# Retention attention followed by a gated feed-forward block: query order, blocks of x^T kept in DRAM, and the order of loads and sums

## The chip, the cores and the metric

The kernel runs on one core of one Trainium2 chip. The core has a matrix engine (PE, TensorE; its weight loads are shown apart as PEld), a vector engine (DVE), a scalar engine (ACT), a general one (POOL, GpSimd) and a queue engine (SP) that issues most DMAs. All run on their own, each through its own instructions in order, and wait for each other by semaphores. The metric is the device time of one execution in microseconds. The kernel before took 1052.0 us (median of 8 runs, 1049.72 to 1055.76).

## What is computed

```python
# q, k, v: (8, 8, 576, 64); w_in: (512, 2048); w_out: (2048, 512)
scores = scale * np.matmul(q, k.transpose(0, 1, 3, 2))
gamma = 1.0 - 2.0 ** (-5.0 - np.arange(H, dtype=np.float32))
rel = pos[:, None] - pos[None, :]
Dmat = np.where(rel >= 0, gamma[:, None, None] ** rel[None, :, :], 0.0)
attn_out = np.matmul(scores * Dmat[None], v)
x = attn_out.transpose(0, 2, 1, 3).reshape(B * S, H * D)      # 4608 x 512
h = x @ w_in
sp = np.maximum(h, 0.0) + np.log1p(np.exp(-np.abs(h)))
g = h * erf(sp)
out = g @ w_out                                               # 4608 x 512
```

The weights come as 64-bit floats, so the kernel reads each as a pair of 32-bit words and makes a 32-bit float of it.

## The kernel before

**Attention.** The 4608 tokens are cut into 36 pieces of 128 tokens: 32 pieces of one batch each, and 4 that hold the last 64 tokens of two batches. Each piece has three stages, written as functions. `transposes(i)` (L300) brings queries and keys into columns: for the first 8 pieces (`SQUARES`) by PE and an ACT copy, later by DVE transposes of 32 x 32 blocks (L310), which read "squares" that the loads have laid out (L115), with token = 4 r + a for row r of block a. It writes both with the tokens in their own order, so the elements of one block lie 4 apart (2 apart in the 64-token pieces). `scores(i)` (L320) multiplies keys and queries and masks them on DVE. `outputs(i)` (L333) multiplies by the values, adds what the state of the batch so far gives, makes the next state (sums on DVE, decay on POOL, L384), and scales the result into the tile `x` (DVE). The values of a piece are first weighed by powers of the decay (`weigh_values`, POOL, L298). The list `stages` (L398) has the order: transposes i+1, outputs i, scores i+1, with two swaps. `attend(upto)` issues the next stages. `load(i, names)` issues the loads of a piece on SP.

**Feed-forward.** Four pieces make a chunk of 512 tokens, 9 chunks. The hidden width is worked through in 4 groups (g = 0 to 3). For each (g, c), `First` multiplies x^T by w_in and `Second` multiplies the result by w_out. Both use a Strassen-Winograd scheme of 7 products instead of 8, each product 4 matmuls of 128 x 128 by 256 (8 records, since a float32 matmul is two). The operands need sums of quarter blocks: S1, S2, S3, S4 of x (`operands_x`, L431; t1 is S1, t2 is S2, t4 stands in the place of A22, S3 takes the place of b12), sums of the weights (L194, L204), and sums of g (`sums`, L532). The first chunk of group 0 is done without the scheme (`plain`). The first group is computed while the attention still delivers x; then x tiles are stored to DRAM (`store_x`, L427; 7 blocks: four of x^T with S3 and three sums) and loaded for groups 1 to 3 (`load_x`, L422). Partial outputs go to DRAM (`od`) and come back in `begin` (L550). Products of a block share PSUM banks: `a` collects product after product, so each must be read (`take`, L568) before the next one is added into it; `e` and `g` hold the others.

**Weights.** `load_weights` issues one part (1/8 of a group, 0.5 MB). `rounding` (L226) makes 32-bit floats of it: two ACT operations, four DVE operations in five steps, two POOL operations (L259, L260), then a new `load_weights`; `round_weights(n)` advances n steps. Four raw buffers.

**Order.** Everything is issued in the order of the Python program. In the beginning a string (L655) has it, one letter a step: a is a stage of attention, p a quarter of half of the plain products, w two parts of weights, a digit so many rounding steps, s `store_x(0)`; after the first stages two dummy matmuls keep PE awake. After that the loop at L679 goes through the blocks First(1), Second(0), First(2), Second(1), ...; a Second block issues products T2, T3, T1 (`middle`), the two products of the First block after next (`first`), then B22 and T4 (`last`), and mixes stages of attention and rounding steps between them.

Of the kernel before, what the change touches and what calls it, by code (L numbers as in the profile page):

```python
# [22 lines left out]
CONST_COLS = H + NP * P + NP + P + H  # L23
# [7 lines left out]
def decays():  # L31

    gamma = 1.0 - 2.0 ** (-5.0 - np.arange(H, dtype=np.float64))
    pairs = gamma.reshape(2, NP)
    t = np.arange(P)
    gk = pairs.T.reshape(1, H) ** -t[:, None]
    row = pairs.repeat(D, axis=0)
    out = np.where(np.arange(NP) % 2 == 0, row, np.roll(row, D, axis=0))  # L40
    gq = out[:, :, None] ** t[None, None, :] / math.sqrt(D)
    gp = row**P
    tri = t[None, :] >= t[:, None]
    gk2 = gk[t % D]
    return np.concatenate([x.reshape(P, -1) for x in (gk, gq, gp, tri, gk2)], axis=1).astype(np.float32)
# [3 lines left out]
def kernel(  # L49
# [39 lines left out]
    xd = [dram.tile([P, n_dc + 3, TCH], FP32, tag="xd", name="xd") for _ in range(n_ch)]  # L89
# [18 lines left out]
    live = {}  # L108

# [45 lines left out]
    nc.scalar.dma_start(out=cst, in_=consts)  # L155
    ends = [0]
    for m in (H, NP * P, NP, P, H):
        ends.append(ends[-1] + m)
    gk, gq, gp, tri, gk2 = (cst[:, a:b] for a, b in zip(ends, ends[1:]))
    gq = gq.rearrange("p (a i) -> p a i", a=NP)  # L160
    gp = gp.unsqueeze(2).to_broadcast([P, NP, D])
    load(1)
    load(2, "kv")
# [62 lines left out]
    def rounding():  # L226


        while True:
            while not words or words[0][2] > most_g[0]:  # L230
                yield
            t, name, g, slot, j, sums = words.pop(0)
            w = operands(name, g)
            dst = w[:, slot : slot + 2, j, :]
            pairs = t[:, :].rearrange("p (h f two) -> p h f two", h=2, two=2)
            pairs_f = t[:, :].bitcast(FP32).rearrange("p (h f two) -> p h f two", h=2, two=2)
            low, high = pairs[:, :, :, 0], pairs[:, :, :, 1]
            r_f, high_f = pairs_f[:, :, :, 0], pairs_f[:, :, :, 1]
            a_f, a = dst, dst.bitcast(UINT32)
            nc.scalar.activation(a_f, high_f, AF.Abs)  # L240
            nc.scalar.mul(out=r_f, in_=low, mul=2.0**-52)
            yield


            nc.vector.tensor_scalar(
                out=a_f, in0=a_f, scalar1=HIGH_LEAST, scalar2=HIGH_MOST, op0=ALU.max, op1=ALU.min
            )
            yield
            nc.vector.tensor_scalar(
                out=a, in0=a, scalar1=3, scalar2=0x3FFFFFFF, op0=ALU.logical_shift_left, op1=ALU.bitwise_and  # L250
            )
            yield
            nc.vector.scalar_tensor_tensor(
                out=a, in0=high, scalar=0xC0000000, in1=a, op0=ALU.bitwise_and, op1=ALU.bitwise_or
            )
            yield

            nc.vector.tensor_scalar(out=high, in0=a, scalar1=0xFF800000, scalar2=None, op0=ALU.bitwise_and)  # L258
            nc.gpsimd.tensor_tensor(out=r_f, in0=high_f, in1=r_f, op=ALU.mult)  # L259
            nc.gpsimd.tensor_tensor(out=a_f, in0=a_f, in1=r_f, op=ALU.add)  # L260
            load_weights()
            yield
            if sums:
                yield from sums(*(w[:, i] for i in range(7)))
# [9 lines left out]

    tri2 = cpool.tile([P, P], FP32, name="tri2")
    nc.vector.tensor_copy(out=tri2, in_=tri)
    nc.vector.memset(tri2[:D, D:], 0.0)

# [21 lines left out]
    def transposes(i):  # L300
        t = live[i] = loaded.pop(i)
        if i < SQUARES:
            weigh_values(i + 1)
        for name in "qk":
            tT = t[name + "T"] = att.tile([P, NP, P], FP32, tag=name + "T", name=name + "T")
            if i >= SQUARES:
                for _, _, n, r0 in pieces[i]:
                    a = r0 // SQ * D
                    squares = t[name + "s"][:, :, a : a + n // SQ * D].rearrange("p h (a d) -> p h a d", d=D)
                    nc.vector.transpose(  # L310
                        out=tT[:, :, r0 : r0 + n].rearrange("p h (r a) -> p h a r", r=SQ), in_=squares[:, :, :, :SQ]
                    )
            else:
                pt = ps_at.tile([P, NP, P], FP32, tag="at", name=f"pt_{name}")
                for p in range(NP):
                    nc.tensor.transpose(pt[:, p, :], flat(t[name][:, 2 * p : 2 * p + 2, :]), ident)
                nc.scalar.copy(out=tT, in_=pt)
        load(i + 2, "q")
# [14 lines left out]
    def outputs(i):  # L333
# [5 lines left out]
        o = [ps_at.tile([P, 4, P], FP32, tag="at", name=f"o{j}") for j in range(2)]  # L339
# [10 lines left out]
        for state, r0, n in seen:  # L350
            for p in range(NP):
                for e in range(2):
                    nc.tensor.matmul(
                        o[p % 2][heads[(e + p) % 2], p // 2, r0 : r0 + n],
                        lhsT=state[heads[e], p, :],
                        rhs=t["qT"][heads[e], p, r0 : r0 + n],
# [4 lines left out]
        b, s0, n, _ = segments[0]  # L361
        if n == P:

            kv = o[0].rearrange("p a i -> p (a i)")[:, 2 * P :].rearrange("p (a d) -> p a d", a=NP)
            for p in range(NP):
                for e in range(2):
# [7 lines left out]
                    )  # L374
            sums = kv
# [9 lines left out]
            kept[b] = new  # L385
        load(i + 3, "kv")
        weigh_values(i + 1)
        c, at = i // PC, i % PC * P
        if (0, c) not in x:
            x[0, c] = x_tile()  # L390
        for j in range(2):
            by = gq[:, j::2, :n].unsqueeze(2).to_broadcast([P, 2, P // n, n])
            dst, got = (
                y.rearrange("p a (m i) -> p a m i", i=n) for y in (x[0, c][:, j:NP:2, at : at + P], o[j][:, :2])
            )
            tt(dst, got, by, ALU.mult)

    stages = [(transposes, 0), (scores, 0)]  # L398
    for i in range(len(pieces)):
        stages += [(transposes, i + 1), (outputs, i), (scores, i + 1)]  # L400
        if i in (PC - 1, PC):
            stages[-3:-1] = stages[-2], stages[-3]
# [19 lines left out]
    def load_x(g, c):  # L422
        m = n_dc + 3 if c > 0 else n_dc
        x[g, c] = x_tile()
        nc.sync.dma_start(out=x[g, c][:, :m], in_=xd[c][:, :m])

    def store_x(c):  # L427
        m = n_dc + 3 if c > 0 else n_dc
        nc.sync.dma_start(out=xd[c][:, :m], in_=x[0, c][:, :m])

    def operands_x(g, c):  # L431
# [3 lines left out]
        if g == 0 or c == 0:  # L435
# [3 lines left out]
            tt(t4, b21, t2, ALU.subtract)  # L439
        if g == 0:  # L440
            store_x(c)
        x[g, c] = {A11: b11, A12: b21, S4: b22, A22: t4, S1: t1, S2: t2, S3: b12}

    class First:
# [87 lines left out]
        def sums(self):  # L532
            g11, g21, g12, g22 = (t[:, j] for t in (self.t1, self.t2) for j in range(2))
            s1, s2, s3, s4 = (self.s[:, i, j] for i in range(2) for j in range(2))
            tt(s1, g12, g22, ALU.add)
            tt(s2, s1, g11, ALU.subtract)
            tt(s3, g11, g12, ALU.subtract)
            tt(s4, g21, s2, ALU.subtract)
# [3 lines left out]
    class Second:  # L542


        def __init__(self, first):
            self.of = first
            self.g, self.c = first.g, first.c
            self.end = (self.g, self.c) == (n_g - 1, n_ch - 1)
# [19 lines left out]
        def take(self, half, oh, acc, engine):  # L568
# [3 lines left out]
            elif engine == "scalar":  # L572
                nc.scalar.copy(out=dst, in_=acc)
            else:
                nc.vector.tensor_copy(out=dst, in_=acc)
# [5 lines left out]
        def first(self):  # L581
# [3 lines left out]
            self.take(0, 0, self.a, "scalar")  # L585
# [5 lines left out]
        def middle(self):  # L591
            self.e = ps_e.tile([P, 2, OH], FP32, tag="g", name="g2")
            self.product(T2, self.a, False)
            self.take(1, 0, self.a, "vector")
# [4 lines left out]
            self.take(1, 1, self.a, "vector")  # L599
# [3 lines left out]
        def last(self):  # L603
            self.product(B22, self.a, False)
            self.take(0, 1, self.a, "scalar")
            self.store(0)
            if self.end:
                self.store(1, slice(OH, D_MODEL))
# [3 lines left out]
            self.store(1, slice(0, OH if self.end else D_MODEL))  # L612
            yield

        def store(self, half, os=slice(0, D_MODEL)):
            if self.g < n_g - 1:
                nc.sync.dma_start(out=od[self.c][:, half, :, os], in_=self.o[:, half, :, os])
            else:
                for tp in range(2):
                    for b, s0, n, r0 in pieces[self.c * PC + 2 * half + tp]:  # L620
                        nc.sync.dma_start(
                            out=out[b * S + s0 : b * S + s0 + n, os], in_=self.o[r0 : r0 + n, half, tp, os]
                        )
# [31 lines left out]
    for j, what in enumerate("aaaawaaawaa4a1a5asa1a4pa5papapa5p4apa1p4apa5a5a"):  # L655
# [4 lines left out]
        elif what == "s":  # L660
            store_x(0)
        elif what == "w":
            load_weights()
            load_weights()
        else:
            round_weights(int(what))
        if j < 7 and what == "a":
            keep_busy(2)
    firsts[0].softplus()
    most[0] = before_chunk(3)  # L670
    attend(after_chunk(1))
    operands_x(0, 1)
    attend(done[0] + 1)
# [4 lines left out]
    firsts[0].multiply()  # L678
    for b, nxt in zip(blocks[1:], blocks[2:] + [None]):  # L679
        n = order.index((b.g, b.c))  # L680
        if isinstance(b, First):
            most_g[0] = order[n - 1][0] + 1
            seconds[n - 1].begin()
            if n + 1 < n_s and order[n + 1][0] > 0:
                load_x(*order[n + 1])
# [5 lines left out]
        elif n + 2 < n_s:  # L691
            f = firsts[n + 1]
            for step, _ in enumerate(b.middle()):
                attend(min(done[0] + 1, most[0]))
                if step == 0:
                    f.erf()
            if n + 2 < n_ch:
                attend(after_chunk(n + 2))
            operands_x(*order[n + 2])
            run(nxt.first(), (1,))  # L700
            f.multiply()
            run(b.last(), (0, 1))
        elif n + 1 < n_s:
            firsts[n + 1].erf()
            seconds[n + 1].begin()
            run(b.middle())
            firsts[n + 1].multiply()
            run(b.last())
            firsts[n + 1].sums()
            run(nxt.first())  # L710
        else:
            run(b.middle())
            run(b.last())
# [30 lines left out]
```

## Time and profile before

| | |
|---|---|
| median of 8 runs | 1052.0 us |
| the profiled execution | 1052.88 us, its span 1051.1 us |
| PE busy | 1023.1 us (97%) |
| weight loads of PE | 878.7 us (84%) |
| DVE busy | 641.6 us (61%) |
| ACT busy | 378.5 us (36%) |
| POOL busy | 133.6 us (13%) |
| moved by DMA | 192.23 MB, mean 183 GB/s |
| store of one x tile | 1792 KB, 8 of them |
| load of one x tile | 1792 KB, 24 of them, median 10.9 us to landing; 3 of 1024 KB, 9.4 us |
| output stores | 43, at most 256 KB, 2.4 us to landing |

The profile is one execution. Busy shares are means over the whole span, and the kernel has stages with different limits, so the shares of a stage and the idle time in front of single instructions say more than the table. In rows of the timeline the bracket at the end is the idle time of the engine before the instruction and what ended it. PE's clock can be granted in part; a matmul then takes longer without any idle time.

### The profile page before, as it was taken

Reading aid. Unit: us, or ns where it says so; the run is one execution under the profiler, and the core shown is the slowest. Engines: PE = TensorE matmul, PEld = TensorE weight load, DVE = VectorE, ACT = ScalarE, POOL = GpSimd, SP = SyncE. Lnnn points to the kernel's source line nnn. Section 1 sums busy time; section 2 is a strip of 40 time slices with the busy share of each in tenths; the row PEclk is TensorE's granted clock in tenths of the full one; section 3 lists DMA queues with packets and bytes.
Section 4 is the critical chain, followed back from the end, with each engine's and each line's share of the span. In section 5 each row is a group of like instructions: output and inputs, shape, how many; then the busy total and the mean of one; then the engine's idle time right before and its main releaser. Section 6 shows DMA issues by size and latency. Waiting matters only on the chain.

```text
span 1051.1 us, 15730 instructions
## 1 busy us (share of the span) xinstructions
PE 1023.1 (97%) x6322; PEld 878.7 (84%) x6322; DVE 641.6 (61%) x1001; ACT 378.5 (36%) x459; POOL 133.6 (13%) x130
## 2 busy tenths in 40 slices
PE   8789999999999999999999999999999999999997
PEld 7668887787788888888888888888888888888885
DVE  3679888778687654556655655555556544454444
ACT  3233232231331444443433333434443333333341
POOL 2551331221221100100001000110100000000000
PEclk9879999999999999999999999999999999999999
DMA  9989979989996534544455455554343444454432
GB/s 195 250 175 242 242 185 256 213 228 238 215 260 177 190 110 150 190 170 170 159 197 198 153 188 206 190 191 150 150 150 121 150 170 176 165 199 174 167 121 80
DMA packets 146777, 192.23 MB, mean 183 GB/s; under 512 B 96016, under 2 KB 121104, under 8 KB 138640
## 3 DMA queue, kind: packets, MB, share of 16 engines
q1 hardware_dynamic: 146560, 190.88, 61.4%
q8 instruction: 50, 0.82, 0.3%
q10 hardware_dynamic: 144, 0.34, 0.1%
q14 instruction: 23, 0.19, 0.1%
HBM read 137.70 MB, written 53.48 MB: 182 GB/s over the span
## 4 chain that ended last, share of the span: by engine, by line
PE 72%; DMA 6%; DVE 6%; SPq 4%; issue 1%; DVEq 0%; ACT 0%
PE a L559 21%; PE a L453 19%; PE g L453 10%; PE g L559 10%; PE e L559 5%; PE e L453 5%; SPq L123 2%; DMA raw_qs<-in_q_dram 2%; DMA raw_v<-in_v_dram 1%; DVE t L93 1%; DMA raw_ks<-in_k_dram 1%; SPq L137 1%; DVE x L93 1%; PE s L326 1%; DVE o L93 1%
## 5 line engine op out<-in xcount | busy, mean ns | idle before, releaser
L453 PE MATMUL a<-x,wa 128*128 128x256 f32 x1120 | 267.8, 382 | 0.0
L453 PEld LDWEIGHTS a<-x,wa 128*128 128x128 f32 x1120 | 212.7, 191 | 29.9 <-issue 0.2
L559 PE MATMUL a<-wb,s 128*128 128x256 f32 x864 | 205.6, 381 | 2.1 <-DVE o L93 2.1
L559 PEld LDWEIGHTS a<-wb,s 128*128 128x128 f32 x864 | 162.9, 190 | 26.1 <-DVE o L93 2.4
L93 DVE TENSOR_TENSOR o<-a,o 128x512 f32<-128x512 f32 x108 | 74.4, 689 | 108.3 <-PE a L559 104.0
L93 DVE TENSOR_TENSOR t<-g,t 128x512 f32<-128x512 f32 x70 | 48.3, 690 | 147.6 <-ACT t L483 112.5
L453 PE MATMUL g<-x,wa 128*128 128x256 f32 x560 | 133.4, 381 | 0.4 <-DVE o L93 0.3
L453 PEld LDWEIGHTS g<-x,wa 128*128 128x128 f32 x560 | 105.5, 190 | 16.4 <-DVE o L93 1.6
L259 POOL TENSOR_TENSOR wraw<-wraw 128x512 f32<-128x512 f32 x32 | 33.5, 1047 | 459.5 <-DVE wraw L258 242.4
L478 ACT COPY t<-a 128x512 f32<-128x512 f32 x35 | 20.5, 587 | 186.8 <-PE a L453 186.8
L93 DVE TENSOR_TENSOR t<-t,s 128x1024 f32<-128x1024 f32 x72 | 87.2, 1253 | 0.0
L522 ACT ACTIVATE s<-t 128x1024 f32<-128x1024 f32 x72 | 72.1, 1049 | 36.3 <-DVE t L93 36.3
L489 ACT COPY t<-a 128x512 f32<-128x512 f32 x35 | 20.5, 586 | 149.7 <-PE a L453 149.7
L559 PE MATMUL g<-wb,s 128*128 128x256 f32 x288 | 69.6, 385 | 3.1 <-DVE t L93 3.1
L526 ACT ACTIVATE s<-s 128x1024 f32<-128x1024 f32 x72 | 72.1, 1049 | 0.4
L559 PE MATMUL a<-wb,t 128*128 128x256 f32 x288 | 68.6, 381 | 0.0
L559 PE MATMUL e<-wb,t 128*128 128x256 f32 x288 | 68.6, 381 | 0.0
L559 PE MATMUL g<-wb,t 128*128 128x256 f32 x288 | 68.2, 380 | 0.0
L453 PE MATMUL e<-x,wa 128*128 128x256 f32 x280 | 66.9, 382 | 0.0
L559 PEld LDWEIGHTS g<-wb,s 128*128 128x128 f32 x288 | 54.9, 192 | 11.0 <-DVE t L93 3.4
L559 PEld LDWEIGHTS g<-wb,t 128*128 128x128 f32 x288 | 54.6, 190 | 7.5
L559 PEld LDWEIGHTS e<-wb,t 128*128 128x128 f32 x288 | 54.3, 190 | 7.7
(77 smaller groups left out, 1175.2 us busy)
## 6 DMA issues: line engine op xcount, KB each, us to landing
x<-xd SPq DMA_DIRECT2D x24, 1792.0 KB, 10.9
od<-o SPq DMA_DIRECT2D x54, 512.0 KB, 4.2
o<-od SPq DMA_DIRECT2D x27, 1024.0 KB, 7.2
xd<-x SPq DMA_DIRECT2D x8, 1792.0 KB, 7.5
raw_qs<-in_q_dram SPq DMA_DIRECT2D x96, 112.0 KB, 5.0
raw_ks<-in_k_dram SPq DMA_DIRECT2D x96, 112.0 KB, 4.5
raw_k<-in_k_dram SPq DMA_DIRECT2D x64, 128.0 KB, 4.5
raw_v<-in_v_dram SPq DMA_DIRECT2D x64, 128.0 KB, 4.7
```

Of the source, the lines that this page charges most:

```text
L93: nc.vector.tensor_tensor(out=out, in0=in0, in1=in1, op=op)
L123: nc.sync.dma_start(out=t[part * SQ : (part + 1) * SQ, :, at : at + m - SQ], in_=tokens[:, :, d0 : d0 + m - SQ])
L137: nc.sync.dma_start(out=t[r0 : r0 + n, e::2, :], in_=heads.rearrange("h p d -> p h d"))
L259: nc.gpsimd.tensor_tensor(out=r_f, in0=high_f, in1=r_f, op=ALU.mult)
L326: nc.tensor.matmul(ps[e][:, p, :], lhsT=t["kT"][heads[e], p, :], rhs=t["qT"][heads[e], p, :], start=True, stop=True)
L453: nc.tensor.matmul(acc[:, j * TH : (j + 1) * TH], lhsT=weights["wa", self.g][:, a, d, j * P : (j + 1) * P], rhs=x[self.g, self.c][a][:, d, :],
L478: nc.scalar.copy(out=self.t1[:, 1], in_=self.a)
L489: nc.scalar.copy(out=self.t2[:, 0], in_=self.a)
L522: nc.scalar.activation(self.s[:, j], t, AF.Softplus)
L526: nc.scalar.activation(self.s[:, j], self.s[:, j], AF.Erf)
L559: nc.tensor.matmul(acc[:, tp, :], lhsT=left[:, j * TH + tp * P : j * TH + (tp + 1) * P], rhs=weights["wb", self.g][:, b, j, :], start=(sta ...
```

## The change

- The queries of a piece keep the order of the squares (a, r) instead of the token order (r, a): DVE transposes and ACT copies write them in a row, mask and query factors (`tri`, `gq`, now also `tri2`, `gq2` for the 64-token pieces) are permuted on the host, x and the output tile hold the tokens in that order, and the last stores put them back: 4 DMAs of 32 rows for one of 128.
- The DRAM tile of x has four blocks instead of seven; t1, t2 and t4 are made again on DVE after each load.
- The constants come in two parts on SP's queue.
- Loads of x and of partial outputs are issued in a Second block ahead of its stores, one block earlier; the sums of a loaded x are made in the second step of `middle`.
- The beginning has a new order of stages, weights (w is one part) and rounding; for group 0 a rounding step issues no new load; the POOL operations of group 0's w_in parts go to DVE; the values of the first 8 pieces are weighed in their own `transposes`.
- In `outputs` the bank o[1] is scaled ahead of the state, o[0] after it.
- The DVE copies of `take` go to ACT. The last two Second blocks run in an order of their own (`rest`), with part of their stores on ACT's queue.

```diff
@@ transposes, outputs
         if i < SQUARES:
-            weigh_values(i + 1)
+            weigh_values(i)
...
+                    order = "p h (a r) -> p h a r" if name == "q" else "p h (r a) -> p h a r"
                     nc.vector.transpose(
-                        out=tT[:, :, r0 : r0 + n].rearrange("p h (r a) -> p h a r", r=SQ), in_=squares[:, :, :, :SQ]
+                        out=tT[:, :, r0 : r0 + n].rearrange(order, r=SQ), in_=squares[:, :, :, :SQ]
                     )
...
-                nc.scalar.copy(out=tT, in_=pt)
+                if name == "q":
+                    nc.scalar.copy(
+                        out=tT.rearrange("p h (a r) -> p h a r", r=SQ), in_=pt.rearrange("p h (r a) -> p h a r", r=SQ)
+                    )
+                else:
+                    nc.scalar.copy(out=tT, in_=pt)
...
+        scaled(1)
+        if n == P:
             sums = kv
...
+        scaled(0)
         load(i + 3, "kv")
-        weigh_values(i + 1)
+        if i + 1 >= SQUARES:
+            weigh_values(i + 1)
...
-        if i in (PC - 1, PC):
+        if i in (PC + 1, 2 * PC - 1):
             stages[-3:-1] = stages[-2], stages[-3]
@@ rounding
-            nc.gpsimd.tensor_tensor(out=r_f, in0=high_f, in1=r_f, op=ALU.mult)
-            nc.gpsimd.tensor_tensor(out=a_f, in0=a_f, in1=r_f, op=ALU.add)
-            load_weights()
+            engine = nc.vector if (name, g) == ("wa", 0) else nc.gpsimd
+            engine.tensor_tensor(out=r_f, in0=high_f, in1=r_f, op=ALU.mult)
+            engine.tensor_tensor(out=a_f, in0=a_f, in1=r_f, op=ALU.add)
+            if g > 0:
+                load_weights()
@@ constants
-    nc.scalar.dma_start(out=cst, in_=consts)
+    nc.sync.dma_start(out=cst[:, :CONST_FIRST], in_=consts[:, :CONST_FIRST])
...
     load(1)
-    load(2, "kv")
@@ x
-    xd = [dram.tile([P, n_dc + 3, TCH], FP32, tag="xd", name="xd") for _ in range(n_ch)]
+    xd = [dram.tile([P, n_dc, TCH], FP32, tag="xd", name="xd") for _ in range(n_ch)]
...
             tt(b12, b22, b12, ALU.subtract)
-            tt(t4, b21, t2, ALU.subtract)
+        else:
+            tt(t2, b12, b11, ALU.add)
+            tt(t1, b22, t2, ALU.subtract)
         if g == 0:
             store_x(c)
+        tt(t4, b21, t2, ALU.subtract)
@@ Second
+        def rest(self):
+            e = ps_e.tile([P, 2, OH], FP32, tag="g", name="g2")
+            self.product(T2, self.a, False)
+            self.take(1, 0, self.a)
+            yield
+            self.product(T3, e, True)
+            self.add(1, 1, e)
+            self.store(0, slice(0, OH), nc.scalar)
+            yield
+            self.product(T1, self.a, False)
+            self.take(1, 1, self.a)
+            yield
+            self.product(T4, e, False)
+            self.add(1, 0, e)
+            self.store(1)
+            yield
+            self.product(B22, self.a, False)
+            self.take(0, 1, self.a)
+            for tp, queue in enumerate((nc.sync, nc.scalar)):
+                self.store(0, slice(OH, D_MODEL), queue, (tp,))
+            yield
...
+                        rows = out[b * S + s0 : b * S + s0 + n, os].rearrange("(r a) o -> a r o", r=SQ)
+                        for a in range(n // SQ):
+                            at = slice(r0 + a * SQ, r0 + (a + 1) * SQ)
+                            queue.dma_start(out=rows[a], in_=self.o[at, half, tp, os])
@@ order of the beginning (l: load(2, "kv"); c: second part of the constants; k: two dummy matmuls)
-    for j, what in enumerate("aaaawaaawaa4a1a5asa1a4pa5papapa5p4apa1p4apa5a5a"):
+    for what in "alkakakawkakakawaa3awwa2aaa5aawwa5pap5ppwwca4pa5pa5paa5ps1":
...
-    attend(after_chunk(1))
+    attend(after_chunk(1) + 1)
     operands_x(0, 1)
-    attend(done[0] + 1)
+    round_weights(4)
@@ loop
             most_g[0] = order[n - 1][0] + 1
-            seconds[n - 1].begin()
-            if n + 1 < n_s and order[n + 1][0] > 0:
-                load_x(*order[n + 1])
+            if n in (1, 2):
+                load_weights()
+                load_weights()
...
                 if step == 0:
                     f.erf()
+                elif step == 1 and n + 2 >= n_ch:
+                    operands_x(*order[n + 2])
             if n + 2 < n_ch:
                 attend(after_chunk(n + 2))
-            operands_x(*order[n + 2])
+                operands_x(*order[n + 2])
             run(nxt.first(), (1,))
             f.multiply()
+            seconds[n + 1].begin()
+            if n_ch <= n + 3 < n_s:
+                load_x(*order[n + 3])
             run(b.last(), (0, 1))
```

## The prediction

> **What bounds the kernel now.** I read the page's slices first, then the busy time by stretch, then the idle time in front of single TensorE (PE) instructions, last the VectorE (DVE) groups by shape.
>
> The page, 40 slices of 26.3 us:
>
> ```profile
> PE   8789999999999999999999999999999999999997
> ...
> DVE  3679888778687654556655655555556544454444
> ...
> PEclk9879999999999999999999999999999999999999
> DMA  9989979989996534544455455554343444454432
> ```
>
> Three stages are to be seen. In the first three slices PE is not full and its granted clock is below one. Up to about 337 us (where the last attention work ends) PE, DVE and DMA are all near full. After that PE alone is full, and in the last slice it is not. By stretch (us, then busy us of PE, PEld, DVE, ACT, POOL, then clock, DMA share, GB/s):
>
> ```profile
> 20.00:40.00 20.00, 14.19 (x168) 11.34 (x168) 11.01 (x24) 7.04 (x12) 9.21 (x10) 0.83 1.08 209
> ...
> 60.00:80.00 20.00, 15.15 (x144) 12.10 (x143) 16.14 (x28) 6.83 (x10) 11.77 (x10) 0.68 0.95 195
> 80.00:100.00 20.00, 20.00 (x197) 16.27 (x200) 19.32 (x31) 7.98 (x11) 1.04 (x1) 0.98 1.16 252
> ...
> 260.00:280.00 20.00, 17.63 (x130) 14.30 (x130) 11.18 (x18) 7.72 (x8) 2.70 (x3) 0.91 1.05 236
> 390.00:440.00 50.00, 50.00 (x234) 44.01 (x233) 25.67 (x40) 21.43 (x27) 2.34 (x2) 1.00 0.45 167
> ```
>
> From 340 to 1025 us every stretch looks like the last row: PE 50 of 50 us, with at most 0.08 us missing in two of them. Nothing can be gained there; it can only be spoiled. So the sum is made of the beginning, the middle (80 to 340 us) and the end. The gaps, in the timeline of PE (start, us, instruction, idle before it and its releaser):
>
> ```profile
> 32.38 1.13 PE L353 MATMUL o<-qT,state 64*64 64x128 f32 x16 [3.42 <-POOL state L384]
> ...
> 67.75 2.57 PE L342 MATMUL o<-sT,raw_v 128*64 128x128 f32 x16 [2.75 <-DVE sT L93]
> 74.53 2.08 PE L326 MATMUL s<-qT,kT 64*128 64x128 f32 x16 [2.10 <-DVE kT L310]
> ...
> 271.04 3.06 PE L559 MATMUL g<-wb,s 128*128 128x256 f32 x8 [2.37 <-DVE t L93]
> ...
> 1041.71 1.99 PE L559 MATMUL a<-wb,s 128*128 128x256 f32 x8 [0.78 <-DVE o L93]
> ```
>
> **Beginning, 0 to 82 us.** Idle over 0.25 us in front of PE: 1.36 + 0.45 + 1.09 + 1.49 + 3.42 + 0.73 + 2.75 + 2.10 = 13.4 us. Cold work is on top: the first row above took 1.13 where the same instructions take 0.67 elsewhere, the second 2.57 for 1.09, the third 2.08 for 1.16. With their neighbours (1.12 for 0.69 twice, two transpose groups, the first products at 76.5 us, 3.78 for 1.9 and 2.17 for 1.75) that is 1.8 us after 32 us and 5.6 us from 68 to 82 us. Here a rule and the rows differ. The Trainium skill, "TensorE: Matmul & The Clock Gate", section "What's actually happening", halves the clock after an idle window of about 3.4 us. By it only the 3.42 us gap would cost speed, 1.8 us. The trace shows 0.50 from 68 to 80 us after a gap of 2.75 us, so I count both, 7.4 us.
>
> What moves there:
> - *Values.* The 3.42 us gap: PE waits for the state (POOL, L384), which stood behind weigh_values (L298) of the next-but-one piece; that multiplication idled 9.30 us until its values landed at 30.7 us. Each piece is now weighed one stage later, and load(2) of keys and values goes behind load(2) of queries (the transposes of piece 2 waited 1.09 us for those). What is late next is the DMA: q and k of piece 4 and 5.
> - *Weights.* Four parts (2 MB) stood ahead of piece 4 and 5; now one stands ahead of k4 and two ahead of k5. Before, 5.3 MB lay up to v4 and landed at 30.7 us, 5.8 us per MB (estimate). k4 needs 4.5 MB, 26 us; k5 5.8 MB, 32 us. So the scores of piece 5 end and the first plain product starts at about 36 to 37 us, against 38.26 us, with one piece more of attention done (17 stages before it instead of 14: transposes, outputs and scores, 1.3 + 2.45 + 1.16 = 4.9 us). Ahead by some 6.5 us.
> - *Rest of it.* From 38.26 to 76.54 us (first product of chunk 1) PE did 30 us of work, the rest was gaps and cold. 25 us remain: 62 us with no gap at all. DVE allows less: it was busy 44 us up to there (4.0 + 11.0 + 16.3 + some 13), and the 8 POOL operations of the first w_in parts come to it, 8 x 0.69 = 5.5 us. Against that, DVE operations of 0.43 us took 1.2 to 1.4 us beside POOL's (68.20, 71.66 us). From 20 us on, 46 us of DVE work: 66 us. Its waits and gaps remain somewhere. I take 68 us, 8.5 us early, and 2.5 us of cold products that become warm: **-11 us** (-4 to -17).
> - The constants go from ACT's queue to SP's behind load(0): issue 0.42 us, needed by the first mask at 9.0 us; 0 to +0.5 us. tri2's copy and memset (0.23 + 0.11 us, in front of an idle DVE) are nothing. The permuted ACT copies of q (8 x 0.586 us) read PSUM 16 bytes apart, which no row shows; 0 to +0.6 us each, on an ACT with 7 us busy in 20: I take 0.
>
> **Middle, 80 to 340 us.** PE's idle there is 0.56 + 0.94 + 0.61 + 0.75 + 0.63 + 2.37 = 5.9 us, all behind DVE, and 1.7 us of cold work after 271 us. DVE is busy 211 of 260 us. It loses:
>
> ```profile
> L310 DVE STREAM_TRANSPOSE qT<-raw_qs 128x512 f32<-128x512 f32 x24 | 26.8, 1116 | 12.3 <-DMA raw_qs<-in_q_dram 12.3
> ...
> L575 DVE COPY o<-a 128x512 f32<-128x512 f32 x18 | 12.4, 686 | 15.9 <-PE a L559 15.9
> ...
> L310 DVE STREAM_TRANSPOSE qT<-raw_qs 128x256 f32<-128x256 f32 x8 | 3.0, 419 | 0.0
> ```
>
> The 512-column transposes write at a stride of 4 elements, the 256-column ones at 2: 2.2 against 1.6 ns an element. q is now written in a row. Between 1116 (no gain) and about 0.64 us (a plain rate), nearest to the stride-2 row: 2 x 419 less a fixed part, 0.79 us. So 24 x 0.33 = 8 us. The 18 COPYs go to ACT (0.59 us each, ACT is below half busy): 12.4 us. Of DMA, 3 of 7 blocks of each x tile go: 0.77 MB x 8 stores = 6.2 MB of some 75 MB up to 340 us, at 230 GB/s 27 us of a queue that is full. Three weight parts (1.5 MB) come in from the beginning. The 2.37 us gap goes back to a transpose that waited 4.87 us for its queries, so both reliefs meet it. I take **-5 us** of the 7.6 (-2 to -7.6).
>
> **Steady stage.** 24 reloaded chunks now make t1, t2 and t4 (operands S1, S2, A22) on DVE: 3 x 0.69 = 2.07 us each, 50 us in sum, beside PE. In the block at 700 us DVE idles 2.76 us in front of the take of product T1 (712.43 us), once the take of product T2 has ended (709.67): the three fit, 0.7 us to spare. What queues behind them: that take, then the add, and PE's B22 product needs it at 715.7 us, so they may be 2.6 us late at no cost. The load (1.0 MB, median 9.4 us to landing in its three rows) may start once chunk n+1's last product ends (707.2) and is needed 26.7 us later, at 733.9. Cost 0 (-0.5 to +1).
>
> The output stores of the last group become 4 DMAs each, 16 a block instead of about 4. A rule speaks against that: "DMA: Bandwidth & Descriptors", "Measured" and "Anatomy of one DMA", says that a DMA costs about 2 us fixed and to batch to 1 MiB. In series, 16 x 2 = 32 us in a block of 24.2: 9 x 8 = 70 us more. The row says otherwise: 43 such DMAs were issued at a median 0.448 us apart while each landed in 2.4 us, so they overlap. 16 x 0.45 = 7.2 us of SP per block, hidden. I take the row.
>
> **End.** The last two blocks' gaps 0.79 + 0.55 + 0.78 = 2.1 us go, since another product stands between a read and its bank's next product. But SP has 8 DMAs from T4's half (from 0.9 us before the last product's end) and then 4 more: the last is issued 4.05 us after that end, where before it was 2.67 us (1048.1 against 1045.43). +1.4 us. Net **-0.7 us** (-2 to +1.5).
>
> **Sum:** -11 - 5 + 0 - 0.7 = -16.7 us. The profiled execution took 1052.88 us (span 1051.1 and 1.8 around it); that gives 1036.2, and from the median of 1052.0, 1035.3. I say **1036 us**.
>
> **Rivals.**
> - *The beginning is bound by supply (15%).* DMA shares are 0.91 to 1.08 in the first 80 us; reordering moves no byte out of attention's way except 1.5 MB of weights. Then only 2 us come there, with middle and end: 1045. Against it: PE's longest gaps there name POOL and DVE, and the x store of 1 MB also goes behind.
> - *All goes (9%).* Gaps and cold work of 0 to 340 us, 11.6 + 7.4 + 5.9 + 1.7 = 26.6 us without the start that stays (1.36 + 0.45), and 0.7: about 1026.
> - *Slower (5%).* The x sums stand at the head of DVE's queue and wait for a late load: then the take, the add and PE's B22 wait too. It decides from 2.6 us of lateness; each further us costs 24 in 24 blocks, so 2 us past it give 1036 + 48 = 1084. For it: SP waited 106.9 us for weight buffers (L223), in front of loads. Against it: a lead of 26.7 us for 9.4.
> - *Nothing seen (3%).* What DVE gains from q and the takes it gives back to the 5.5 us of POOL work, and PE waits as before: 1051.
>
> **Numbers.** Forecast 68%. The ends of its parts, all added on one side, give 1026 and 1049; the range 1027 to 1046 leaves out the outermost of these, takes in the first rival and stops a microsecond short of the second. A difference of 0.2% (2.1 us) is what this kernel's measurement tells from none. Faster: 0.68 + 0.15 + 0.09 = 0.92; same 0.03; slower 0.05.
>
> **What would show it.** First product of chunk 1 at about 68 us, clock 0.9 or more from 60 to 80 us; no POOL-released gap near 32 us. qT rows of 512 near 0.8 us, kT still 1.1. Fewer than 3 us of PE gaps from 80 to 340 us; attention ended near 321 us. No gap from 340 to 1025 us, x rows x3 inside DVE's idle time. The last out store issued about 4 us after the last product. A first product of chunk 1 after 74 us, or gaps in front of B22, would make me wrong.

## The result, and the profile after

The changed kernel takes 1044.5 us (median of 11 runs, 1043.2 to 1049.5), the kernel before 1052.6 us (32 runs, 1049.4 to 1055.8). The ratio is 0.9929 with a 95% interval of 0.9917 to 0.9942: 7.5 us less. The forecast was 16 us less. The profiled execution took 1045.46 us, its span is 1043.7 us against 1051.1 us.

The slices of the page of the changed kernel, to be laid beside those of before:

```profile
PE   8887999999999999999999999999999999999997
...
DVE  3996778778767645567655656666657655555554
...
PEclk9998999999999999999999999999999999999999
DMA  9989879998994531643264523363333334443433
```

The clock of the second and third slice is better and PE's second slice is fuller, but the fourth, full before at a clock of 9, now shows 7 at a clock of 8. What was won early was lost again there. To see how much, I take one mark in each block: the start of the second product of each `Second` block (`e<-wb,t` on PE), and subtract the same mark of the kernel before (us, one profiled execution each; S0 is Second(0), the last is S35):

```
            S0    S1    S2    S3    S4    S5    S6   ...  S16  ...  S34   S35   last mark to end
before    95.0 136.1 175.8 220.0 259.3 301.6 338.9        580.7     1016.5 1033.1     18.0
change    -8.5  -1.3  +0.4  -2.2  -2.4  -6.5  -6.5         -5.7      -6.4  -7.4     18.1
```

So there are four parts: 8.5 us won up to S0 (13.1 us up to the first product of chunk 1, which starts at 63.47 us and not at 76.54), nearly all of it lost between S0 and S1; 5.2 us won from S1 to S5; blocks of 24.17 us as before in the steady stage (0.8 us lost in three blocks after S6 come back at the two changes of group); 1.0 us in the last block. PE's timeline in the changed kernel, at the gaps over half a microsecond from 60 us on:

```profile
66.15 1.16 PE L335 MATMUL s<-qT,kT 64*128 64x128 f32 x16 [0.69 <-DVE kT L314]
...
72.53 1.64 PE L353 MATMUL o<-sT,raw_v 128*64 128x128 f32 x16 [1.57 <-issue]
...
78.65 1.16 PE L335 MATMUL s<-qT,kT 64*128 64x128 f32 x16 [1.94 <-DVE kT L314]
79.74 3.68 PE L469 MATMUL a<-x,wa 128*128 128x256 f32 x8
...
94.02 2.08 PE L335 MATMUL s<-qT,kT 64*128 64x128 f32 x16 [5.46 <-DVE kT L314]
```

After 94 us there is none until the end. The largest, 5.46 us, is in First(1)'s stretch, and names DVE's key transposes. DVE's own timeline just before shows that the transposes were not what was late:

```profile
90.56 0.43 DVE L251 TENSOR_SCALAR wa<-wa 128x512 f32<-128x512 f32 x1 [6.83 <-ACT wa L246]
91.59 0.69 DVE L99 TENSOR_TENSOR t<-g,t 128x512 f32<-128x512 f32 x1 [0.60 <-ACT t L499]
92.20 0.70 DVE L314 STREAM_TRANSPOSE qT<-raw_qs 128x512 f32<-128x512 f32 x1
92.83 1.04 DVE L314 STREAM_TRANSPOSE kT<-raw_ks 128x512 f32<-128x512 f32 x1
```

DVE stood 6.83 us in front of a rounding step of weights (L251). The transposes were queued behind it and one sum (L99), and had no wait of their own. ACT's timeline has the next link, and SP's issue the one after:

```profile
89.87 0.66 ACT L246 ACTIVATE wa<-wraw 128x512 f32<-128x512 f32 x1 [18.28 <-DMA wraw<-in_moe_w_in_dram]
90.43 0.66 ACT L247 ACTIVATE wraw<-wraw 128x512 f32<-128x512 uint32 x1
90.99 0.57 ACT L499 COPY t<-a 128x512 f32<-128x512 f32 x1
```

```profile
82.95 2.48 SPq L229 DMA_DIRECT2D wraw<-in_moe_w_in_dram  x4
```

The two parts of group 1 that First(1) now loads were issued at 82.95 us (SP was busy with squares up to there) and took a median of 6.5 us to land. The rounding step that is next in the program needs the first of them at once. ACT takes its instructions in order, so it waited 18.3 us, some 11 of them before the load was even issued, and behind it stood two copies of products (91.0 and 91.5 us). In the kernel before, a part was loaded four parts ahead: SP issued the first loads of group 1 from 59.87 us on, and ACT read one at 86.37 us without any wait.

```profile
59.87 1.20 SPq L223 DMA_DIRECT2D wraw<-in_moe_w_in_dram  x2
...
86.37 0.68 ACT L240 ACTIVATE wa<-wraw 128x512 f32<-128x512 f32 x1
```

### The profile page after: what moved, and what is told of

It reads as the page before. It is cut to its first block, busy times and chain, and to the rows that moved or that the text cites. A ratio compares the mean times of both kernels' runs of the same rounds, so it can differ in the third digit from the quotient of the medians.

```text
span 1043.7 us, 15938 instructions
## 1 busy us (share of the span) xinstructions
PE 1019.2 (98%) x6322; PEld 875.8 (84%) x6322; DVE 674.0 (65%) x1061; ACT 388.0 (37%) x477; POOL 124.7 (12%) x122
## 4 chain that ended last, share of the span: by engine, by line
PE 89%; DMA 3%; SPq 3%; DVE 2%; issue 1%; ACT 1%; DVEq 0%; ACTq 0%
PE a L576 23%; PE a L469 23%; PE g L469 12%; PE g L576 12%; PE e L576 6%; PE e L469 6%; PE s L335 3%; PE o L353 3%; SPq L144 2%; PE o L376 1%; PE o L364 1%; DMA wraw<-in_moe_w_in_dram 1%; DMA raw_qs<-in_q_dram 1%; SPq L130 1%; DVE x L99 1%
## 5 line engine op out<-in xcount | busy, mean ns | idle before, releaser
L99 DVE TENSOR_TENSOR t<-g,t 128x512 f32<-128x512 f32 x70 | 48.3, 691 | 156.2 <-ACT t L499 116.0
L99 DVE TENSOR_TENSOR o<-a,o 128x512 f32<-128x512 f32 x108 | 74.3, 688 | 50.4 <-PE a L576 50.4
L99 DVE TENSOR_TENSOR t<-t,s 128x1024 f32<-128x1024 f32 x72 | 87.4, 1254 | 0.0
L266 POOL TENSOR_TENSOR wraw<-wraw 128x512 f32<-128x512 f32 x28 | 29.1, 1041 | 456.2 <-DVE wraw L264 244.4
L99 DVE TENSOR_TENSOR x<-x 128x512 f32<-128x512 f32 x116 | 77.9, 704 | 1.2
L99 DVE TENSOR_TENSOR o<-g,o 128x512 f32<-128x512 f32 x72 | 49.4, 686 | 27.3 <-ACT o L590 22.5
L99 DVE TENSOR_TENSOR sT<-s,cst 128x512 f32<-128x512 f32 x72 | 46.2, 682 | 25.5 <-PE s L335 25.3
```

Source lines behind the costliest of these rows:

```text
L99: nc.vector.tensor_tensor(out=out, in0=in0, in1=in1, op=op)
L266: engine.tensor_tensor(out=r_f, in0=high_f, in1=r_f, op=ALU.mult)
```

## The experiments

Theory A: the loss from S0 to S1 is this wait. Theory B: the DMA queue limits that stretch, and the wait only stands in for it. All ratios are to the kernel before, on the same chip. Single traces of one program differ by some microseconds, so what an edit is worth is read from the ratios and their 95% intervals, and the marks only show where.

**e1: the loads earlier.** The first two parts of group 1 are issued at the end of the string.

```diff
-..."pa5pa5paa5ps1"
+..."pa5pa5paa5pwws1"
-            if n in (1, 2):
+            if n == 2:
```

> The changed kernel, but the first two weight parts of group 1 are loaded at the end of the string of the beginning (ahead of store_x(0)) and not in First(1). Theory A (the 15 us gained up to chunk 1 are lost between 67 and 108 us because ACT waits 18.3 us for a weight part issued at 82.95 us, DVE waits 6.8 us behind it, and PE 5.46 us at 94.02 us, and then runs cold): the gap at 94 us goes, about 8 us faster than the changed kernel, some 1036 us against 1052 before. Theory B (the DMA queue is what limits 67 to 108 us; queries and keys of pieces 10 and 11 come no earlier, and 1 MB more ahead of them makes it worse): 1044 or slower, with gaps in front of the scores of pieces 10 and 11.

Measured: 1041.97 us, ratio 0.9921 (0.9905 to 0.9936). The gap at 94 us is gone and S1 comes 11.0 us before that of the kernel before (the change: 1.3). But S2 comes only 2.9 us before it: a new gap, and cold work after it.

```profile
159.51 1.08 DVE L314 STREAM_TRANSPOSE kT<-raw_ks 128x512 f32<-128x512 f32 x1 [3.06 <-DMA raw_ks<-in_k_dram]
...
160.74 2.08 PE L335 MATMUL s<-qT,kT 64*128 64x128 f32 x16 [2.88 <-DVE kT L314]
```

Here the transposes do wait for their squares. SP's queue says why these came late:

```profile
137.60 4.34 SPq L130 DMA_DIRECT2D raw_qs<-in_q_dram  x8
142.04 4.15 SPq L130 DMA_DIRECT2D raw_ks<-in_k_dram  x8
146.29 2.59 SPq L144 DMA_DIRECT2D raw_v<-in_v_dram  x4
...
151.53 2.45 SPq L130 DMA_DIRECT2D raw_ks<-in_k_dram  x4
...
142.00:150.00 8.00, 8.00 (x80) 6.43 (x80) 5.08 (x10) 2.31 (x4) 0.79 (x1) 1.00 0.40 92
```

The loads of a piece of two batches are 20 small DMAs (48 and 64 KB), and SP issued them without a break for 11.3 us. Meanwhile the DMA engines were busy 0.40 of the time (the last line, 142 to 150 us, the figure before GB/s). The keys that the transpose at 159.51 us waited for stood behind them in SP's order (151.53 us), and from 150 us on the engines were full again (1.07). So two limits follow each other there: SP's issues, then the bytes. e2, e8 and e13 show the same 20 issues at the same place.

**e2: the rounding later.** The loads stay, the four rounding steps of First(1)'s stretch are made in First(2)'s.

```diff
-            run(b.middle(), (1, 1))
+            m = {1: 0, 2: 2}.get(n, 1)
+            run(b.middle(), (m, m))
...
-            run(seconds[n - 1].first(), (1, 1))
+            run(seconds[n - 1].first(), (m, m))
```

> The changed kernel, but the four rounding steps of First(1)'s stretch are made in First(2)'s (two at a time); the loads stay where they are. Theory A: ACT has nothing to wait for at 89.9 us, the 5.46 us gap goes, 6 to 8 us faster than the changed kernel (1036 to 1038). Theory B: no difference (1044), since the transposes wait for their squares all the same.

Measured: 1041.27 us, ratio 0.9911 (0.9897 to 0.9925). S1 11.2 us before, S2 2.8 us, with a gap of 3.07 us at 162 us. e1 and e2 take the wait away from two sides (in e1, 2.5 us of it stay on ACT, at 73.86 us) and do the same: A is right about the gap, and what B says comes true one block later. About 8 and 6 to 8 us were expected; against the changed kernel the ratios give 1 and 2 us, and their intervals overlap with its own.

**w1: the late loads alone, put into the kernel before.**

```diff
-            load_weights()
+            if g > 0 or name == "wa":
+                load_weights()
...
+            if n in (1, 2):
+                load_weights()
+                load_weights()
             seconds[n - 1].begin()
```

> The kernel before with one edit of the change alone: no load of a group 1 part out of group 0's w_out rounding; two parts are loaded in First(1) and two in First(2) instead. Theory A (the rounding step right behind its load makes ACT, then DVE, then PE wait): a gap of some us in front of scores in First(1)'s or Second(0)'s stretch (85 to 110 us), Second(1) 4 to 9 us later than in the kernel before, the end 2 to 8 us slower. If 2 MB less in the stream of the beginning outweighs it: the first product of chunk 1 earlier and the end at 1052 within 2 us.

Measured: 1061.68 us, ratio 1.0105 (1.0086 to 1.0125): 11 us slower, more than expected. ACT waits 12.8 us for the part, S1 is 7.7 us late, S2 11.3, and from S5 on it stays at 11.2 to the end. The chain is the same, from ACT's copy to PE (what ended the second gap, the last line, the profile does not name):

```profile
97.75 0.66 ACT L240 ACTIVATE wa<-wraw 128x512 f32<-128x512 f32 x1 [12.82 <-DMA wraw<-in_moe_w_in_dram]
98.31 0.66 ACT L241 ACTIVATE wraw<-wraw 128x512 f32<-128x512 uint32 x1
98.87 0.56 ACT L484 COPY t<-a 128x512 f32<-128x512 f32 x1
```

```profile
99.48 1.99 PE L454 MATMUL a<-x,wa 128*128 128x256 f32 x8 [2.79 <-ACT t L484]
104.38 1.90 PE L343 MATMUL o<-sT,raw_v 128*64 128x128 f32 x15 [2.90 <-issue]
```

**c1: the changed kernel again**, beside e4, e8 and e10.

> The changed kernel itself, so that the others are compared with it on the same chip: ratio to before 0.993 as on record, within 0.0015 by every theory.

Measured: 1044.74 us, ratio 0.9935 (0.9915 to 0.9956); S0, S1 and S5 are -8.0, -1.2 and -7.0 us.

**e8: less in the stream.** e2, with a quarter of each x tile stored and read four times over.

```diff
-        nc.sync.dma_start(out=x[g, c][:, :n_dc], in_=xd[c])
+        nc.sync.dma_start(out=x[g, c][:, :n_dc], in_=xd[c].to_broadcast([P, n_dc, TCH]))
...
-        nc.sync.dma_start(out=xd[c], in_=x[0, c][:, :n_dc])
+        nc.sync.dma_start(out=xd[c], in_=x[0, c][:, :1])
```

> e2 (rounding late), but only one of the four blocks of an x tile is stored, and each load reads that block four times, so the later groups compute with other values of x; nothing else is changed. Theory B' (what e1 and e2 gained at the first chunk is lost between 125 and 173 us since squares come no faster than the DMA stream, which is busy without a break from 60 to 145 us): 0.77 MB less in front of pieces 9, 11 and 17, 3.3 us each at 230 GB/s, so the gap of 2.9 to 3.1 us before the scores of piece 18 near 161 us goes and Second(2) comes 5 to 8 us earlier than in e2; end some 5 us earlier than e2. Theory C (DVE and PE order, not the stream, sets that stretch): the gap stays and the time is e2's within 1 us.

Measured: 1036.88 us, ratio 0.9859 (0.9836 to 0.9881), 5.5 us less than e2 by the ratios. S2 is 7.4 us before the kernel before, S5 14.9. The gap near 160 us is 2.4 us and does not go; SP's 20 issues are still there (engines busy 0.42 from 141 to 149 us). So bytes in the stream are time somewhere up to S5, but they are not all of what is lost; that they are what is lost between S1 and S2 is not shown (see e13).

**e4: more in the stream.** The changed kernel with seven blocks stored and loaded again.

```diff
-        nc.sync.dma_start(out=xd[c], in_=x[0, c][:, :n_dc])
+        m = n_dc + 3 if c > 0 else n_dc
+        nc.sync.dma_start(out=xd[c][:, :m], in_=x[0, c][:, :m])
...
```

> The changed kernel with seven blocks of an x tile in DRAM again, loaded as they are (t1, t2, t4 not made again after a load). DVE has 50 us less work after 340 us. Theory B': 0.77 MB more in each chunk's stream, up to 3.3 us a chunk where the stream is the limit: 3 to 10 us slower than the changed kernel, with gaps in front of scores between 140 and 300 us. Theory C: the same within 1 us. The prediction's steady step (sums hidden at no cost) says that the blocks from 370 to 1000 us stay at 24.17 us either way.

Measured: 1058.07 us, ratio 1.0064 (1.0042 to 1.0087), 13.5 us slower than the changed kernel beside it, where 3 to 10 were expected. The weight part lands later still and the gap at 94 us becomes the first line below; others follow up to 341 us. S1 to S5 are +1.1, +4.8, +7.4, +8.6 and +6.1 us. From S7 to S34 the marks stay where they are within 0.7 us: the sums that DVE is spared there give nothing, as the prediction had it.

```profile
96.79 2.08 PE L335 MATMUL s<-qT,kT 64*128 64x128 f32 x16 [9.71 <-DVE kT L314]
...
186.81 1.40 PE L353 MATMUL o<-sT,raw_v 128*64 128x128 f32 x16 [2.56 <-POOL raw_v L301]
```

**e3: the values in the old order.**

```diff
-            weigh_values(i)
+            weigh_values(i + 1)
...
-        if i + 1 >= SQUARES:
-            weigh_values(i + 1)
+        weigh_values(i + 1)
```

> The changed kernel with weigh_values(i + 1) again in the first transposes and in every outputs. If POOL's wait for the next piece's values makes the gap near 32 us (prediction's step on values), PE shows a POOL-released gap of some us between 25 and 45 us again; whether the end moves depends on the later gap: by theory A the beginning has about 8 us to spare in front of the weight wait at 90 us, so the time stays at 1044 within 1; by theory B (supply) it stays too. If the values' order is on the path to the end, 2 to 4 us slower.

Measured: 1046.09 us, ratio 0.9956 (0.9941 to 0.9971), about 2.5 us slower. The gap is back, 2.97 us at 30.65 us behind POOL's state, and all later marks are 2 to 3 us late. That there was time to spare in front of the weight wait was wrong: SP's issues slip along with it, the weight part among them (86.48 us instead of 82.95).

**e5: the token order**, queries, masks and stores as before the change.

```diff
-        i = np.arange(n).reshape(-1, n // 32).T.reshape(-1)
+        i = np.arange(n)
...
-                    order = "p h (a r) -> p h a r" if name == "q" else "p h (r a) -> p h a r"
+                    order = "p h (r a) -> p h a r"
...
```

> The changed kernel with queries in the token order again: transposes and copies as before, unpermuted mask and factors, one output DMA for a piece. Prediction's step: DVE loses 24 x 0.33 = 8 us less there; qT rows of 512 back at 1.1 us; 2 to 5 us slower through the middle (108 to 306 us), and the last stores shorter by about 1.4 us. If the query order does nothing for the path (DVE has slack once 6.2 MB of DMA and the takes are gone): the same or 1 us faster through the shorter tail.

Measured: 1041.24 us, ratio 0.9918 (0.9902 to 0.9934): not the 2 to 5 us slower that the prediction's step would make it; the ratio is 1 to 2 us better, which its interval does not tell from none. The tail is 3.4 us shorter (14.7 us from the last mark to the end, 18.1 in the changed kernel), and the middle is not longer (S1 to S5 -5.2 us, as in the change).

**e12: whole stores, squares' order kept.** One DMA for a piece, so the rows of the output stay permuted.

> The changed kernel with queries in the squares' order, but the output of a piece stored by one DMA, so the rows of out stay in the squares' order and are not put back. Shows the stores by themselves, without the transposes that e5 also changed: tail 3.3 us shorter as in e5, blocks of group 4 unchanged at 24.17 us, everything up to 1020 us as in the changed kernel. About 3 us faster.

Measured: 1041.95 us, ratio 0.9913 (0.9896 to 0.9930). The tail is 14.7 us, as in e5. The four-fold stores thus cost 3.3 us in the tail of these traces; e5 and e12 differ by less than their intervals, so no gain of the query order shows.

**e11: the last stores on two queues.**

```diff
-            self.store(1)
+            for tp, queue in enumerate((nc.sync, nc.scalar)):
+                self.store(1, queue=queue, tps=(tp,))
```

> The changed kernel, but in the last two blocks the 8 stores of T4's half go half to SP's and half to ACT's queue. If the last 4 stores wait for the 8 in front of them on SP (last issue 4.65 us after the last product's end, 2.67 before the change): last issue near 2.2 us after it, tail from the last product to the end 7.5 us down to 5 to 5.5, 2 to 2.5 us faster than the changed kernel. If the landing of small stores sets the tail: within 0.5 us.

Measured: 1042.93 us, ratio 0.9919 (0.9900 to 0.9938). The tail is 15.7 us from the last mark, 2.4 us less. The ratio alone can't tell the gain from none.

**e10 and e13: together.** e10 is e2 with e5, e13 is e2 with e11.

> e2 and e5 together: rounding late, queries in token order, one output DMA for a piece. If the two gains (each about 1.5 to 2 us against the changed kernel by ratio) are of different places (the weight wait in the beginning, the stores in the tail), they add: some 3.5 to 4.5 us faster than the changed kernel. If DVE's longer transposes (24 x 0.4 us) then decide the stretch from 125 to 175 us, the sum is less than either and Second(2) is late.

> e2 and e11 together (rounding late, last stores on two queues), queries in the squares' order: 1.9 + 2.3 us faster than the changed kernel if they add, ratio to before some 0.989; e10 (token order instead) had 0.988. If the query order is worth its 1.7 us of e2 against e10 at the last block, this one is 1 us faster than e10.

Measured: e10 1039.40 us, ratio 0.9881 (0.9857 to 0.9906); e13 1037.36 us, ratio 0.9873 (0.9853 to 0.9893). Both beat the two kernels; e13 is some 6 us below the changed one. The two can't be told apart, though e10's tail is 1.0 us shorter: with the wait gone, a gain of the query order of a microsecond or two is neither shown nor excluded. One caution comes from e13: up to the last blocks it is e2, yet its S2 is 8.3 us before the kernel before where e2's was 2.8. Part of it is the clock: after the gap near 160 us e1 and e2 have 0.66 and 0.83 from 160 to 170 us, e13 and e8 1.00. Between S1 and S2 single executions thus differ by 5 us, and e8's lead over e2 at S2 may be no more than that. What I say of bytes rests on the ratios of e4 and e8 over the whole time, not on one trace.

## Why the prediction was wrong

The sum of the prediction had 16.7 us, the kernel gained 7.5: some 9 us are missing, all of them between the first product of chunk 1 and S5. Two things failed, a wait that was put at nothing and the adding of two terms that share one limit.

- **Beginning, -11 us: the mechanism was right and larger, and then a new wait ate it.** The POOL gap at 32 us is gone (e3 brings it back), the clock from 60 to 80 us is 0.99, and what is late at 32 us is q and k of piece 5, as forecast:

```profile
32.00 0.63 PE L320 MATMUL pt_q<-ident,raw_q 128*128 128x128 f32 x4 [1.72 <-DMA raw_q<-in_q_dram]
...
36.27 1.99 PE L523 MATMUL p<-x,wa 128*128 128x256 f32 x8
```

  The first plain product starts at 36.27 us (forecast 36 to 37; by the prediction's own rate 5.8 MB are 34 us, not the 32 it wrote), that of chunk 1 at 63.47 (forecast 68). The failed step is one sentence of the middle: "Three weight parts (1.5 MB) come in from the beginning." It prices the moved loads as bytes and not as a wait, and does not ask which instruction is next behind them. It is the rounding of that very part, on ACT, in order. At S1 1.3 us were left; with the wait taken away 11 are there (e1, e2). w1 prices this edit alone at 11 us in the kernel before. In the changed kernel, taking it away is worth less at the end: by the ratios 1 us (e1), 2 (e2), 4 (e10 against e5) and 5 (e13 against e11). Each ratio is known to 1.3 to 2.6 us, so only the last two are clear of none. The signs that were to show the prediction wrong, a late chunk 1 or gaps in front of B22, did not come: the loss was at a place for which it had named none.
- **That the terms add** was the second thing taken for granted. With the wait gone, 8 us of the 11 at S1 are lost again by S2 in e1 and e2, and 3 in e13. From S1 to S5 the changed kernel, late at S1, gains 5.2 us; e1 and e2, early there, gain nothing (+0.3 and +0.7). At S5, where the sum has 16, the changed kernel has 6.5, e1 and e2 10.7 and 10.5, e13 13.6. The supply of squares, values, weights and stores is the limit there: 0.77 MB a chunk more cost 13.5 us (e4), 0.77 MB less brought 5.5 (e8), and near 145 us it is SP's issues and not the bytes (e1's trace). No run changed the number of these issues, so how much of the loss is theirs stays open. The first rival (bound by supply) named this limit and its 1045 is nearly the time measured, but that is luck: it put the limit in the first 80 us, where 13 us were won.
- **Middle, -5 us:** -5.2 measured from S1 to S5, but not for the reason that led the sum, and in part by luck, since a kernel that had not lost its lead gains nothing there. DVE's relief was there (qT rows of 512 at 0.70 us, forecast 0.79; kT 1.10), yet e5 gives it back without loss. The four blocks count: with seven, the same stretch loses 5.0 us (e4). What the 18 copies moved to ACT brought, no run shows. Attention ended at 329 us, forecast 321 (before 335).
- **Steady stage, 0:** right. Blocks take 24.17 us, no gap of PE is over 0.22 us from 340 us on, and the three x sums lie in DVE's idle time between two takes, with 0.83 us to spare (forecast 0.7):

```profile
702.94 0.69 DVE L99 TENSOR_TENSOR o<-a,o 128x512 f32<-128x512 f32 x1 [1.03 <-PE a L576]
703.55 2.01 DVE L99 TENSOR_TENSOR x<-x 128x512 f32<-128x512 f32 x3
706.40 0.69 DVE L99 TENSOR_TENSOR o<-a,o 128x512 f32<-128x512 f32 x1 [0.83 <-PE a L576]
```

- **The rule on batching DMAs against the row:** the row held. Sixteen output stores were issued in 7.37 us of a 24.17 us block, and the blocks of the last group did not grow. The two sections of "DMA: Bandwidth & Descriptors" that the prediction names speak of DMAs issued by GpSimd, and these stores are issued by SP and ACT, so the rule was stretched from the start. What small stores cost shows only at the tail.
- **End, -0.7 us:** -1.0 measured, but both terms were too small and their errors cancel. PE's last two blocks, from S34 to the end of the last product, are 2.9 us shorter (forecast 2.1 from the gaps that went). From that end to the end of the kernel it takes 7.5 us instead of 5.7, 1.9 us more (forecast 1.4); the last store is issued 4.6 us after it (forecast 4.05).

## What to carry to other kernels

When a load is moved later, look for the first instruction that reads it, and list what is queued behind that instruction on its engine; bytes alone do not price the move. A gain in a stage that feeds a saturated stage should be followed block by block to the end before it is counted: here 13 us at 63 us were 1.3 us at the second mark, and gains of two stages with one limit did not add. Where a gap names one engine, go back link by link (PE, DVE, ACT, DMA, issue) before believing the name. A queue can be the limit by its issues while the DMA engines are half idle, so both are to be read.

## What was not expected of the hardware

The same gap did not always cost clock. A PE gap of 1.94 us at 78.65 us was followed by products at half speed in the changed kernel (3.68 us for 1.9), and by full speed in e2 (gap 1.95 us) and in e11, which is the changed kernel itself up to its last blocks:

```profile
79.48 1.16 PE L335 MATMUL s<-qT,kT 64*128 64x128 f32 x16 [1.95 <-DVE kT L314]
80.57 1.99 PE L469 MATMUL a<-x,wa 128*128 128x256 f32 x8
```

The gap of 2.75 us from which the prediction took 5.6 us of cold work is in w1 too (at 69.32 us). There the two groups behind it ran at full speed, 0.67 and 0.69 us where the kernel before took 1.13 and 1.12:

```profile
70.94 0.67 PE L354 MATMUL o<-qT,state 64*64 64x128 f32 x16
71.53 0.69 PE L368 MATMUL o<-raw_v,raw_k 128*64 128x64 f32 x16
...
70.00:80.00 10.00, 7.92 (x76) 6.65 (x77) 9.83 (x17) 0.94 (x2) 6.14 (x5) 0.83 0.70 156
```

The clock from 70 to 80 us was 0.83 there and 0.50 in the kernel before. So cold work after gaps of 2 to 3 us differs from execution to execution, and the 5.6 us were no fixed term. The Trainium skill ("TensorE: Matmul & The Clock Gate", "What's actually happening") asks for an idle window of about 3.4 us and would let none of these gaps cost anything; the rows differ from that. Its remark that the window is free-running fits such a difference between executions, but no run here shows the window itself.
